# Moving one FFN multiply to GpSimd, reordering FFN pairs around the kv groups, and splitting small loads, in a fused linear-attention and SwiGLU kernel

## The chip, the cores and the metric

The kernel runs on one core of a Trainium2 chip. Its time is in device microseconds. Engines: PE is TensorE (matmuls), PEld its weight loads, DVE VectorE, ACT ScalarE, POOL GpSimd, SP SyncE. "Span" is the time from the first to the last instruction in a trace; the timed result is about 1.8 us longer. A program on one core has no second die to compare with; the runs used below are those marked "fast", and where it matters I also give the granted TensorE clock of the run, as a share of full speed.

## The reference, cut to what matters

```python
g = sigmoid((x * gate_w).sum(-1))                 # x: 2048 x 640
qkv = x @ wqkv                                    # 32 heads of 20
phi(t) = [softmax(t @ w_phi), softmax(-t @ w_phi)]
kv = phi(k)^T v ; z = sum(phi(k))                 # over all 2048 tokens
a = (phi(q) @ kv / (phi(q) @ z + 1e-6)) @ wo
b = (silu(x @ w_gate) * (x @ w_up)) @ w_down      # FFN, 1728 wide
out = g * a + (1 - g) * b
```

## The kernel before

The program has these stages. **Start:** wqkv (k part) is multiplied with a block-diagonal wbd, built from 36 small w_phi loads. **Phase 1:** for 16 token tiles, exp of both signs of the k features (`ek`), v, and the softmax normalisation of `ek`, done by POOL. **kv groups:** twelve PSUM accumulations over all 16 tiles. **Four blocks of 512 tokens:** pq chunks (q features, two exps each), zw (denominators), exp/psi items (DVE multiplies `eq` by a broadcast in PSUM, which a matmul with the weights `gtm` makes), oT chunks (attention output, evicted by ACT), then the final products with wo and wd. FFN work, in units called pairs (14 per block: gate matmuls, up matmuls, and the elementwise part), is spread between all these as filler.

A helper adds the semaphore waits from the tiles that an operation reads and writes. In the stretches shown below each engine's instructions start in the order in which the program issues them. FFN and pq outputs take turns on a ring of four PSUM banks (0 to 3); items and oT chunks alternate between banks 4 and 5.

```python
for i, (h, m1, p1, e0, e1) in enumerate(blk):                  # 36 small loads
    dma("act" if (i % 3 == 2) else "pool", dst, src)
dma("act", wvg[:, :, 0:D], ...)                                # 800 KB
...
for t in range(NT):                                            # phase 1
    ...                                                        # 20 matmuls, 2 exps, v copies
    for sg in range(2):                                        # DVE sum, reciprocal, then:
        poolop(lambda: pool.tensor_tensor(eka, eka, rb, ALU.mult), ...)
...
def ffn_pair(bt, k):             # and ffn_half(bt, k, which), the same in two halves
    mm_group(gap, [(wg[:, c, P*k:P*k+rk], xT[:, c, tsl]) for c in range(5)])
    mm_group(uap, [(wu[:, c, P*k:P*k+rk], xT[:, c, tsl]) for c in range(5)])
    actop(hap, gap, ACTF.Tanh, scale=0.5)
    dveop(... hap = (hap + 1.0) * gap ...)         # scalar_tensor_tensor, gap in PSUM
    dveop(... hap = (hap * 0.5) * uap ...)         # scalar_tensor_tensor, uap in PSUM
...
for k in range(6):
    kv_group(*kvg.pop(0))
    kv_group(*kvg.pop(0))
    ffn_pair(0, k)
...
for bt in range(NBT):
    halves = [(k, w) for k in range(6 if bt == 0 else 0, 14) for w in range(2)]
    # nh() emits the next half, if any is left
    pq_chunk 0, pq_chunk 1, nh(), pq_chunk 2, nh(), ... pq_chunk 5, nh(), nh()
    zw_groups, zw_ops, 4 x nh(), zw_transposes, 2 x nh()
    12 exp_psi_items, nh() after every second one
    6 ot_chunks, nh() after each
    while halves: nh()
    u_loop(bt, buf)              # wo and wd matmuls, combine, store
```

The softmax here doesn't subtract the row's maximum and nothing guards it: scores larger than these inputs give would overflow.

Of the kernel before, what the change touches and what calls it, by code (L numbers as in the profile page):

```python
# [6 lines left out]
P = 128  # L7
# [9 lines left out]
ACTF = mybir.ActivationFunctionType  # L17
ALU = mybir.AluOpType
AX = mybir.AxisListType
DT = mybir.dt  # L20
BF16 = DT.bfloat16
# [170 lines left out]
def _build(  # L192
# [11 lines left out]
    dbg=None,  # L204
):
    tr = _Tracker(nc)
    pe, act, dve, pool, sp = nc.tensor, nc.scalar, nc.vector, nc.gpsimd, nc.sync
# [7 lines left out]
    def sb(name, shape, dtype):  # L215
        t = nc.alloc_sbuf_tensor(name, list(shape), dtype)
        addr = nc.lookup_mloc(t).addr
        tr.reg_tensor(t, "sbuf", addr, shape_rowelems(shape), mybir.dt.size(dtype))
        return t
# [6 lines left out]
    wg = sb("wg", [P, 5, F_FFN], BF16)  # L226
    wu = sb("wu", [P, 5, F_FFN], BF16)
    hT = sb("hT", [P, 14, 512], BF16)
    gtm = [sb("gtm0", [P, 6, 120], BF16), sb("gtm1", [P, 6, 120], BF16)]
    msk = sb("msk", [P, 126], F32)  # L230
    SZW = sb("SZW", [P, 2, 6, 64], BF16)
# [2 lines left out]
    gs = sb("gs", [P, 2, NT], F32)  # L234
# [47 lines left out]
    def bank(b, c0, c1, rows=128):  # L282
        return ps[0:rows, b * 512 + c0: b * 512 + c1]
# [7 lines left out]
    def dma(engname, dst, src, transpose=False):  # L291
        eobj = tr.engobj[engname]

        def fn():
            if transpose:
                return eobj.dma_start(dst, src, transpose=True)
            return eobj.dma_start(dst, src)  # L297
        reads = [src] if src.tensor.name in tr.addr else []
        writes = [dst] if dst.tensor.name in tr.addr else []
        return run(engname, fn, reads=reads, writes=writes, semname="dma")  # L300

    def mm_group(out_ap, pairs):
        reads = [p[0] for p in pairs] + [p[1] for p in pairs]

        def fn():
            n = len(pairs)
            last = None
            for i, (l, r) in enumerate(pairs):
                last = pe.matmul(out_ap, lhsT=l, rhs=r, start=(i == 0), stop=(i == n - 1))  # L309
            return last  # L310
        return run("pe", fn, reads=reads, writes=[out_ap])
# [6 lines left out]
    def actop(out_ap, in_ap, func, scale=1.0):  # L318
        reads = [in_ap]
        if isinstance(scale, bass.AP):  # L320
            reads = reads + [scale]

        def fn():
            return act.activation(out_ap, in_ap, func, scale=scale)  # L324
        return run("act", fn, reads=reads, writes=[out_ap])

    def dveop(fn, reads, writes):
        return run("dve", fn, reads=reads, writes=writes)

    def poolop(fn, reads, writes):  # L330
        return run("pool", fn, reads=reads, writes=writes)

    def memset(t_ap, val, eng="pool"):
        eobj = pool if eng == "pool" else dve
        return run(eng, lambda: eobj.memset(t_ap, val), reads=[], writes=[t_ap])  # L335
# [18 lines left out]
    for i, (h, m1, p1, e0, e1) in enumerate(blk):  # L354
        dst = wbd[p1:p1 + (e1 - e0), m1, DH * h:DH * h + DH]
        src = wphi[h, e0:e1, :]
        dma("act" if (i % 3 == 2) else "pool", dst, src)
    dma("act", wvg[:, :, 0:D], A_wqkv[:, 2 * D:3 * D].rearrange("(c p) j -> p c j", p=P))
    gate_ap = bass.AP(gate_w.tensor, gate_w.offset, [[1, P], [P, 5], [1, 1]])
    with nc.allow_non_contiguous_dma(reason="gate_w column load (640 elems)"):  # L360
# [116 lines left out]
    def ring_next():  # L477
        i = ring_ctr[0] % 4
        ring_ctr[0] += 1
        return i  # L480

    def nrows_f(k):
        return 128 if k < 13 else 64

    def ffn_pair(bt, k):
        tsl = slice(512 * bt, 512 * bt + 512)
        rk = nrows_f(k)
        rg = ring_next()
        gap = bank(rg, 0, 512, rows=rk)
        mm_group(gap, [(wg[:, c, P * k:P * k + rk], xT[:, c, tsl]) for c in range(5)])  # L490
        ru = ring_next()
        uap = bank(ru, 0, 512, rows=rk)
        mm_group(uap, [(wu[:, c, P * k:P * k + rk], xT[:, c, tsl]) for c in range(5)])
        hap = hT[0:rk, k, :]
        actop(hap, gap, ACTF.Tanh, scale=0.5)
        dveop(lambda hap=hap, gap=gap: dve.scalar_tensor_tensor(
            out=hap, in0=hap, scalar=1.0, in1=gap, op0=ALU.add, op1=ALU.mult),
            [hap, gap], [hap])
        dveop(lambda hap=hap, uap=uap: dve.scalar_tensor_tensor(
            out=hap, in0=hap, scalar=0.5, in1=uap, op0=ALU.mult, op1=ALU.mult),  # L500
            [hap, uap], [hap])

    def kv_group(c, sg):
        nr, nk = _nr(c), _nk(c)
        ncol = 21 * nk
# [15 lines left out]
        z1 = oav[:, :, DH:DH + 1]  # L521
        dveop(lambda zdst=zdst, z0=z0, z1=z1: dve.tensor_tensor(zdst, z0, z1, ALU.mult),
              [z0, z1], [zdst])

    kvg = [(c, sg) for c in range(6) for sg in range(2)]
    for k in range(6):
        kv_group(*kvg.pop(0))
        kv_group(*kvg.pop(0))
        ffn_pair(0, k)
    assert not kvg  # L530
    if dbg is not None:
        dump_names1 = ["d_ek", "d_v1", "d_krec", "d_kvsb", "d_SZW", "d_gs"]
    else:
        dump_names1 = []

    def dump_list(names):
        if dbg is None:
            return
        dmap = {
            "d_xT": lambda: xT[:, :, :],  # L540
            "d_wqk": lambda: wqk[:, :, :, :],
            "d_wvg": lambda: wvg[:, :, :],
            "d_ek": lambda: ek[:, :, :, :],
            "d_v1": lambda: v1[:, :, :],
            "d_krec": lambda: krec[:, :, :, :],
            "d_gs": lambda: gs[:, :, :],
            "d_kvsb": lambda: kvsb[0:40, :, 0:40],
            "d_SZW": lambda: SZW[0:120, :, 0:5, :],
            "d_c36": lambda: c36[0:64, :, :],
            "d_hT": lambda: hT[0:64, :, :],  # L550
            "d_eq": lambda: eq[0:40, :, :, :, :],
            "d_oT": lambda: oT[0:40, :, :, :],
            "d_ag": lambda: ag[:, :, :],
        }
        for name in names:
            if name in dbg:
                ev = dma("sp", dbg[name], dmap[name]())
                out_evs.append(ev)
    dump_list(dump_names1)

    for bf_ in range(2):
        memset(oT[:, bf_, 5, :], 0.0)
        for sg in range(2):
            memset(eq[:, bf_, sg, 5, :], 0.0)
    memset(c36[:, :, :], 0.0)

    zwv = ps[0:P, 6 * 512:7 * 512].rearrange("p (u s c) -> p u s c", u=4, s=2)
    sub_ctr = [0]
# [73 lines left out]
    def ffn_half(bt, k, which):  # L642
        tsl = slice(512 * bt, 512 * bt + 512)
        rk = nrows_f(k)
        if which == 0:
            rg = ring_next()
            gap = bank(rg, 0, 512, rows=rk)
            mm_group(gap, [(wg[:, c, P * k:P * k + rk], xT[:, c, tsl]) for c in range(5)])
            ffn_half.gate[k] = gap
            return  # L650
        gap = ffn_half.gate[k]
        ru = ring_next()
        uap = bank(ru, 0, 512, rows=rk)
        mm_group(uap, [(wu[:, c, P * k:P * k + rk], xT[:, c, tsl]) for c in range(5)])
        hap = hT[0:rk, k, :]
        actop(hap, gap, ACTF.Tanh, scale=0.5)
        dveop(lambda hap=hap, gap=gap: dve.scalar_tensor_tensor(  # L657
            out=hap, in0=hap, scalar=1.0, in1=gap, op0=ALU.add, op1=ALU.mult),
            [hap, gap], [hap])
        dveop(lambda hap=hap, uap=uap: dve.scalar_tensor_tensor(  # L660
            out=hap, in0=hap, scalar=0.5, in1=uap, op0=ALU.mult, op1=ALU.mult),
            [hap, uap], [hap])
    ffn_half.gate = {}

    def u_loop(bt, buf):
        for u in range(4):
# [33 lines left out]
    def pq_chunk(bt, buf, m):  # L700
# [5 lines left out]
        actop(eq[0:nr, buf, 0, m, :], oap, ACTF.Exp, scale=1.0)  # L706
        actop(eq[0:nr, buf, 1, m, :], oap, ACTF.Exp, scale=-1.0)

    for bt in range(NBT):
        buf = bt % 2  # L710
        par = bt % 2
        if bt == 0:
            halves = [(k, w) for k in range(6, 14) for w in range(2)]
        else:
            halves = [(k, w) for k in range(14) for w in range(2)]

        def nh():
            if halves:
                ffn_half(bt, *halves.pop(0))

        pq_chunk(bt, buf, 0)
        pq_chunk(bt, buf, 1)
        nh()
        pq_chunk(bt, buf, 2)
        nh()
        pq_chunk(bt, buf, 3)
        nh()
        pq_chunk(bt, buf, 4)
        nh()
        pq_chunk(bt, buf, 5)  # L730
        nh(); nh()
        zw_groups(bt, buf)
        zw_ops(par)
        nh(); nh(); nh(); nh()
        zw_transposes(par)
        nh(); nh()
        items = [(sg, m) for sg in range(2) for m in range(6)]
        for it_i, it in enumerate(items):
            exp_psi_item(bt, buf, par, *it)
            if it_i % 2 == 1:  # L740
                nh()
        for m in range(6):
            ot_chunk(bt, buf, m)
            nh()
        while halves:
            nh()
        u_loop(bt, buf)
# [53 lines left out]
```

## Time and profile before

Median 386.57 us of five runs (386.07 to 388.99). The profiled execution has a span of 384.8 us.

| read from the trace of before | value |
|---|---|
| first PE matmul | 19.16 us |
| first phase-1 matmul | 27.95 us |
| PE idle before the first kv group | 3.45 us |
| exp/psi stretch of blocks 1 to 3 (first gtm to first oT matmul) | 11.47 us each |
| block 0, last oT stretch (first oT to first wo matmul) | 4.68 us |

The page of before gives busy time and share of the span by engine; in its slices each digit is the busy share in tenths of one fortieth of the span, and PEclk is the granted clock in tenths.

```profile
PE 344.2 (89%) x2165; PEld 178.8 (46%) x2201; DVE 171.9 (45%) x302; ACT 127.3 (33%) x244; POOL 72.0 (19%) x105
PE   0099999879999979999989999999999999999996
...
PEclk9999999989999999999999999999999999999999
```

PE is the busy engine, so what matters is where it waits. The waits of PE, before (total us, times, longest):

```profile
PE ps L309 <- DMA wbd<-in_A_w_phi_dram: 19.2, 1, 19.2
PE ps L309 <- DVE eq L626: 5.1, 21, 1.0
PE ps L309 <- POOL ek L468: 3.4, 1, 3.4
PE ps L309 <- DVE hT L657: 2.5, 9, 0.4
PE ps L309 <- ACT oT L324: 1.1, 3, 0.7
```

The start, the exp/psi items (DVE eq), the last normalisation of phase 1 (POOL ek), the first DVE step of the FFN, and the oT evictions. The timeline of PE around the wait for POOL (start us, duration, what, count, idle before):

```profile
74.27 1.53 PE L309 MATMUL ps<-wvg,xT 128*128 128x500 bf16 x10
79.24 2.85 PE L309 MATMUL ps<-v,ek 128*120 128x126 bf16 x32 [3.45 <-POOL ek L468]
82.31 1.91 PE L309 MATMUL ps<-xT,wg 128*128 128x512 bf16 x4 [0.22 <-issue]
84.02 1.16 PE L309 MATMUL ps<-xT,wu 128*128 128x512 bf16 x4
```

From the first gate matmul on record (one of the five is missing) to the first up matmul are four matmuls and 1.71 us, 82.31 to 84.02: 0.43 us per matmul, where the same group of five later takes 1.08 us, 0.215 each. The clock by stretch says why (the number after the POOL entry is the mean granted clock):

```profile
80.00:82.00 2.00, 1.86 (x23) 1.72 (x22) 0.35 (x2) 0.00 (x0) 0.42 (x1) 0.71 0.00 0
82.00:84.00 2.00, 1.78 (x5) 0.64 (x5) 0.35 (x2) 0.00 (x0) 0.00 (x0) 0.50 0.00 0
```

DVE in block 2's exp/psi items runs without a gap:

```profile
262.09 0.69 DVE L657 SCALAR_TENSOR_TENSOR hT<-hT,ps 128x512 bf16<-128x512 bf16 x1 [0.88 <-ACT hT L324]
262.81 0.69 DVE L660 SCALAR_TENSOR_TENSOR hT<-hT,ps 128x512 bf16<-128x512 bf16 x1
263.42 2.55 DVE L626 TENSOR_TENSOR eq<-eq,ps 120x512 bf16<-120x512 bf16 x4
265.88 0.68 DVE L657 SCALAR_TENSOR_TENSOR hT<-hT,ps 128x512 bf16<-128x512 bf16 x1
```

Two FFN steps and four items take 3.79 us (262.09 to 265.88), and so does each group of four items; PE's own work in that time is 3.0 us (four items at 0.215, two halves at 1.08).

### The profile page before, as it was taken

To read this page: it belongs to the slowest core of one execution; us is meant where nothing else is said; L and a number is where in the kernel's file an instruction comes from. 1 tells how busy PE (TensorE), PEld (TensorE's weight loads), DVE (VectorE), ACT (ScalarE), POOL (GpSimd) and SP (SyncE) were. 2 spreads that over 40 slices of the span, in tenths; PEclk is the share of its full clock that TensorE was granted. 3 is DMA by queue.
4 is the path that set the end of the run, shared out by engine and by line. 5 is a ranking of instruction groups with operands and counts; after the bars stand their busy time and mean duration, and the time that the engine had idled before them with its cause. 6 is when DMAs were issued, how large, how long until landed. Compare 5 with 4: busy or idle time off the path is not lost.

```text
span 384.8 us, 5409 instructions
## 1 busy us (share of the span) xinstructions
PE 344.2 (89%) x2165; PEld 178.8 (46%) x2201; DVE 171.9 (45%) x302; ACT 127.3 (33%) x244; POOL 72.0 (19%) x105
## 2 busy tenths in 40 slices
PE   0099999879999979999989999999999999999996
PEld 0045565456644325554434455443445554434554
DVE  0006776744516850123894411268750122894311
ACT  0136777711262241143215212522341143215210
POOL 9996888830300000000000000000000000000000
PEclk9999999989999999999999999999999999999999
DMA  4999664100000000100000010000000000000001
GB/s 98 233 184 237 213 174 122 53 0 2 2 0 2 0 2 17 36 18 0 2 0 1 2 36 34 0 2 0 2 1 19 34 17 2 0 2 0 2 34 36
DMA packets 29525, 15.53 MB, mean 40 GB/s; under 512 B 19325, under 2 KB 29501, under 8 KB 29501
## 3 DMA queue, kind: packets, MB, share of 16 engines
q1 hardware_dynamic: 27097, 14.34, 14.6%
q10 hardware_dynamic: 1636, 0.83, 0.9%
q8 instruction: 18, 0.29, 0.3%
q0 software_dynamic: 768, 0.02, 0.1%
q14 instruction: 6, 0.05, 0.0%
HBM read 8.30 MB, written 2.62 MB: 28 GB/s over the span
## 4 chain that ended last, share of the span: by engine, by line
PE 74%; DVE 13%; ACT 5%; POOL 4%; issue 2%; DMA 1%; POOLq 0%
PE ps L309 73%; DVE eq L626 7%; DVE hT L657 4%; POOL wbd L297 3%; DVE hT L660 2%; ACT eq L324 2%; ACT hT L324 2%; DMA wbd<-in_A_w_phi_dram 1%; PE pst L315 1%; POOL wbd L335 1%; ACT oT L324 1%; POOL ek L468 1%; ACT ek L324 0%; DVE ocomb L694 0%; ACT wqk L324 0%
## 5 line engine op out<-in xcount | busy, mean ns | idle before, releaser
L309 PE MATMUL ps<-xT,wg 128*128 128x512 bf16 (+1 forms) x269 | 68.2, 383 | 3.2 <-DVE hT L657 2.1
L309 PE MATMUL ps<-xT,wu 128*128 128x512 bf16 (+1 forms) x273 | 69.1, 380 | 0.4
L324 ACT ACTIVATE hT<-ps 128x512 bf16<-128x512 f32 (+1 forms) x56 | 33.4, 596 | 90.4 <-PE ps L309 90.4
L309 PE MATMUL ps<-wd,hT 128*128 128x128 bf16 (+1 forms) x440 | 62.5, 297 | 0.4
L657 DVE SCALAR_TENSOR_TENSOR hT<-hT,ps 128x512 bf16<-128x512 bf16 (+1 forms) x50 | 34.2, 684 | 62.9 <-ACT hT L324 62.9
L694 DVE SCALAR_TENSOR_TENSOR ocomb<-ps,gs,ag 128x640 bf16<-128x640 f32 x16 | 14.1, 884 | 78.8 <-PE ps L309 78.8
L309 PEld LDWEIGHTS ps<-wd,hT 128*128 128x128 bf16 x448 | 35.1, 98 | 26.5
L465 DVE TENSOR_REDUCE ksum<-ek 128x32 f32<-128x640 bf16 x32 | 25.3, 791 | 42.5 <-ACT ek L324 42.5
L309 PEld LDWEIGHTS ps<-xT,wu 128*128 128x128 bf16 (+1 forms) x280 | 27.3, 99 | 32.5 <-issue 3.0
L468 POOL TENSOR_TENSOR ek<-ek,krec 128x640 bf16<-128x640 bf16 x32 | 39.9, 1269 | 10.5 <-ACT gtan L324 10.5
L309 PEld LDWEIGHTS ps<-xT,wg 128*128 128x128 bf16 (+1 forms) x280 | 25.9, 99 | 34.0 <-PE ps L309 5.7
L324 ACT ACTIVATE eq<-ps 120x512 bf16<-120x512 f32 (+1 forms) x48 | 26.0, 593 | 29.4 <-PE ps L309 29.4
L660 DVE SCALAR_TENSOR_TENSOR hT<-hT,ps 128x512 bf16<-128x512 bf16 (+1 forms) x50 | 34.3, 686 | 1.7
L324 ACT ACTIVATE ag<-ps,gs 128x640 bf16<-128x640 f32 x16 | 12.7, 793 | 64.8 <-PE ps L309 64.8
L309 PE MATMUL ps<-wbd,wqT 128*128 128x320 bf16 (+2 forms) x65 | 13.6, 352 | 19.2 <-DMA wbd<-in_A_w_phi_dram 19.2
L626 DVE TENSOR_TENSOR eq<-eq,ps 120x512 bf16<-120x512 bf16 (+1 forms) x48 | 30.5, 680 | 0.0
L309 PE MATMUL ps<-wo,oT 120*128 120x512 bf16 (+3 forms) x188 | 28.6, 297 | 1.3 <-ACT oT L324 0.7
L309 PE MATMUL ps<-xT,wqk 128*120 128x512 bf16 (+1 forms) x120 | 29.2, 379 | 0.0
L324 ACT ACTIVATE ek<-ps 128x640 bf16<-128x640 f32 x32 | 20.8, 701 | 14.4 <-PE ps L309 14.4
L309 PE MATMUL ps<-wvg,xT 128*128 128x500 bf16 (+1 forms) x160 | 24.5, 299 | 0.0
L309 PE MATMUL ps<-wqk,xT 128*128 128x512 bf16 (+1 forms) x154 | 23.4, 296 | 1.2 <-ACT wqk L324 0.9
L324 ACT ACTIVATE oT<-ps 120x512 bf16<-120x512 f32 (+1 forms) x24 | 14.3, 596 | 23.3 <-PE ps L309 23.3
(59 smaller groups left out, 252.4 us busy)
## 6 DMA issues: line engine op xcount, KB each, us to landing
out_dram<-ocomb SPq DMA_DIRECT2D x16, 160.0 KB, 1.8
wg<-in_B_w_gate_dram SPq DMA_DIRECT2D x4, 540.0 KB, 4.3
wu<-in_B_w_up_dram SPq DMA_DIRECT2D x4, 540.0 KB, 3.8
wd<-in_B_w_down_dram SPq DMA_DIRECT2D x1, 2080.0 KB, 12.8
wvg<-in_A_wqkv_dram ACTq DMA_DIRECT2D x1, 800.0 KB, 7.2
wo<-in_A_wo_dram SPq DMA_DIRECT2D x1, 750.0 KB, 6.7
wbd<-in_A_w_phi_dram POOLq DMA_DIRECT2D x18, 0.8 KB, 4.5
wqT<-in_A_wqkv_dram SPq DMA_TRANSPOSE x10, 3.4
```

What stands on the lines that cost most here:

```text
L297: return eobj.dma_start(dst, src)
L309: last = pe.matmul(out_ap, lhsT=l, rhs=r, start=(i == 0), stop=(i == n - 1))
L315: return pe.transpose(out_ap, in_ap, ident[:, :])
L324: return act.activation(out_ap, in_ap, func, scale=scale)
L335: return run(eng, lambda: eobj.memset(t_ap, val), reads=[], writes=[t_ap])
L465: dveop(lambda eka=eka, sa=sa: dve.tensor_reduce(sa, eka, AX.X, ALU.add), [eka], [sa])
L468: poolop(lambda eka=eka, rb=rb: pool.tensor_tensor(eka, eka, rb, ALU.mult), [eka, ra], [eka])
L626: dveop(lambda ea=ea, oap=oap: dve.tensor_tensor(ea, ea, oap, ALU.mult), [ea, oap], [ea])
L657: dveop(lambda hap=hap, gap=gap: dve.scalar_tensor_tensor(out=hap, in0=hap, scalar=1.0, in1=gap, op0=ALU.add, op1=ALU.mult), [hap, gap], [ ...
L660: dveop(lambda hap=hap, uap=uap: dve.scalar_tensor_tensor(out=hap, in0=hap, scalar=0.5, in1=uap, op0=ALU.mult, op1=ALU.mult), [hap, uap], ...
L694: dveop(lambda oc=oc, b_ap=b_ap, omg=omg, aga=aga: dve.scalar_tensor_tensor(out=oc, in0=b_ap, scalar=omg, in1=aga, op0=ALU.mult, op1=ALU.add),
```

## The change

Its intent: take the second FFN step off DVE (ACT copies the up result out of PSUM, POOL multiplies in SBUF), use FFN work to cover the wait for the last normalisation, keep more FFN filler for block 0, and share the small loads evenly between two issuing engines.

```diff
+    us2 = sb("us2", [P, 2, 512], BF16)
...
-        dma("act" if (i % 3 == 2) else "pool", dst, src)
+        dma("act" if (i % 2 == 1) else "pool", dst, src)
...          # in ffn_half; ffn_pair now calls ffn_half twice
+        usa = us2[0:rk, k % 2, :]
         actop(hap, gap, ACTF.Tanh, scale=0.5)
+        actop(usa, uap, ACTF.Copy, scale=0.5)
         dveop(... hap = (hap + 1.0) * gap ...)
-        dveop(... hap = (hap * 0.5) * uap ...)
+        poolop(lambda: pool.tensor_tensor(hap, hap, usa, ALU.mult), ...)
...
-    for k in range(6):
-        kv_group(*kvg.pop(0))
-        kv_group(*kvg.pop(0))
-        ffn_pair(0, k)
+    ffn_pair(0, 0)
+    ffn_pair(0, 1)
+    for k in range(2, 8):
+        kv_group(*kvg.pop(0))
+        kv_group(*kvg.pop(0))
+        if k == 4:
+            ffn_pair(0, 2)
...
-            halves = [(k, w) for k in range(6, 14) for w in range(2)]
+            halves = [(k, w) for k in range(3, 14) for w in range(2)]
```

More of the change, by code (lines that the diff above doesn't have):

```diff
@@ L483, in nrows_f @@
         return 128 if k < 13 else 64
-    def ffn_pair(bt, k):
-        tsl = slice(512 * bt, 512 * bt + 512)
-        rk = nrows_f(k)
-        rg = ring_next()
-        gap = bank(rg, 0, 512, rows=rk)
-        mm_group(gap, [(wg[:, c, P * k:P * k + rk], xT[:, c, tsl]) for c in range(5)])
-        ru = ring_next()
-        uap = bank(ru, 0, 512, rows=rk)
-        mm_group(uap, [(wu[:, c, P * k:P * k + rk], xT[:, c, tsl]) for c in range(5)])
-        hap = hT[0:rk, k, :]
-        actop(hap, gap, ACTF.Tanh, scale=0.5)
-        dveop(lambda hap=hap, gap=gap: dve.scalar_tensor_tensor(
-            out=hap, in0=hap, scalar=1.0, in1=gap, op0=ALU.add, op1=ALU.mult),
-            [hap, gap], [hap])
-        dveop(lambda hap=hap, uap=uap: dve.scalar_tensor_tensor(
-            out=hap, in0=hap, scalar=0.5, in1=uap, op0=ALU.mult, op1=ALU.mult),
-            [hap, uap], [hap])
     def kv_group(c, sg):
@@ L523, in kv_group @@
               [z0, z1], [zdst])
-    kvg = [(c, sg) for c in range(6) for sg in range(2)]
-    for k in range(6):
-        kv_group(*kvg.pop(0))
-        kv_group(*kvg.pop(0))
-        ffn_pair(0, k)
-    assert not kvg
-    if dbg is not None:
-        dump_names1 = ["d_ek", "d_v1", "d_krec", "d_kvsb", "d_SZW", "d_gs"]
-    else:
-        dump_names1 = []
-    def dump_list(names):
-        if dbg is None:
-            return
-        dmap = {
-            "d_xT": lambda: xT[:, :, :],
-            "d_wqk": lambda: wqk[:, :, :, :],
-            "d_wvg": lambda: wvg[:, :, :],
-            "d_ek": lambda: ek[:, :, :, :],
-            "d_v1": lambda: v1[:, :, :],
-            "d_krec": lambda: krec[:, :, :, :],
-            "d_gs": lambda: gs[:, :, :],
-            "d_kvsb": lambda: kvsb[0:40, :, 0:40],
-            "d_SZW": lambda: SZW[0:120, :, 0:5, :],
-            "d_c36": lambda: c36[0:64, :, :],
-            "d_hT": lambda: hT[0:64, :, :],
-            "d_eq": lambda: eq[0:40, :, :, :, :],
-            "d_oT": lambda: oT[0:40, :, :, :],
-            "d_ag": lambda: ag[:, :, :],
-        }
-        for name in names:
-            if name in dbg:
-                ev = dma("sp", dbg[name], dmap[name]())
-                out_evs.append(ev)
-    dump_list(dump_names1)
-    for bf_ in range(2):
-        memset(oT[:, bf_, 5, :], 0.0)
-        for sg in range(2):
-            memset(eq[:, bf_, sg, 5, :], 0.0)
-    memset(c36[:, :, :], 0.0)
     zwv = ps[0:P, 6 * 512:7 * 512].rearrange("p (u s c) -> p u s c", u=4, s=2)
@@ L659, in ffn_half, with ffn_pair @@
             [hap, gap], [hap])
-        dveop(lambda hap=hap, uap=uap: dve.scalar_tensor_tensor(
-            out=hap, in0=hap, scalar=0.5, in1=uap, op0=ALU.mult, op1=ALU.mult),
-            [hap, uap], [hap])
+        poolop(lambda hap=hap, usa=usa: pool.tensor_tensor(hap, hap, usa, ALU.mult),
+               [hap, usa], [hap])
     ffn_half.gate = {}
+    def ffn_pair(bt, k):
+        ffn_half(bt, k, 0)
+        ffn_half(bt, k, 1)
     def u_loop(bt, buf):
@@ L707, in pq_chunk, with dump_list @@
         actop(eq[0:nr, buf, 1, m, :], oap, ACTF.Exp, scale=-1.0)
+    kvg = [(c, sg) for c in range(6) for sg in range(2)]
+    ffn_pair(0, 0)
[5 more added lines that the diff above has]
+            ffn_pair(0, 2)
+    assert not kvg
+    if dbg is not None:
+        dump_names1 = ["d_ek", "d_v1", "d_krec", "d_kvsb", "d_SZW", "d_gs"]
+    else:
+        dump_names1 = []
+    def dump_list(names):
+        if dbg is None:
+            return
+        dmap = {
+            "d_xT": lambda: xT[:, :, :],
+            "d_wqk": lambda: wqk[:, :, :, :],
+            "d_wvg": lambda: wvg[:, :, :],
+            "d_ek": lambda: ek[:, :, :, :],
+            "d_v1": lambda: v1[:, :, :],
+            "d_krec": lambda: krec[:, :, :, :],
+            "d_gs": lambda: gs[:, :, :],
+            "d_kvsb": lambda: kvsb[0:40, :, 0:40],
+            "d_SZW": lambda: SZW[0:120, :, 0:5, :],
+            "d_c36": lambda: c36[0:64, :, :],
+            "d_hT": lambda: hT[0:64, :, :],
+            "d_eq": lambda: eq[0:40, :, :, :, :],
+            "d_oT": lambda: oT[0:40, :, :, :],
+            "d_ag": lambda: ag[:, :, :],
+        }
+        for name in names:
+            if name in dbg:
+                ev = dma("sp", dbg[name], dmap[name]())
+                out_evs.append(ev)
+    dump_list(dump_names1)
+    for bf_ in range(2):
+        memset(oT[:, bf_, 5, :], 0.0)
+        for sg in range(2):
+            memset(eq[:, bf_, sg, 5, :], 0.0)
+    memset(c36[:, :, :], 0.0)
     for bt in range(NBT):
```

## The prediction

> **What bounds it now.** TensorE: 344 of 384.8 us busy, and it carries 74% of the chain of waits. It loses time in four places.
> (a) Start: nothing until 19.16 us, waiting for the last small wbd load (longest PE wait, 19.2 us).
> (b) Between phase 1 and the kv groups: the timeline shows PE's last phase-1 matmuls around 75.8 us and the first kv group at 79.24, the second at 80.47, each waiting for a POOL normalisation of ek. Afterwards matmuls are slow: 128x512 matmuls start 0.43 us apart at 82.3 to 84 us, against 0.215 later. This agrees with the Trainium skill, "TensorE: Matmul & The Clock Gate", Part 1 (half clock after an idle window).
> (c) The exp/psi stretch of each token block: DVE alternates hT and eq work without a gap (block 2: DVE 11.8 of 12.0 us at 262 to 274), PE waits for eq.
> (d) Block 0's six oT chunks without FFN filler: PE and ACT alternate, 139.4 to 144.1 us.
>
> **What changes.** wbd loads: POOL issues 18 instead of 24 (0.51 us each), ACT 18 instead of 12 (about 0.46). FFN: the second DVE step (0.69 us, x56) becomes an ACT copy (0.6 us) plus a POOL multiply; ek's multiply on POOL takes 1.27 us for 640 columns, so I estimate 1.05 us for 512. POOL is idle then. The skill ("GPSIMD Engine Reference", 3.1) calls two-input work there about twice as slow as on DVE; off the chain that costs little. Order: two FFN pairs before the kv groups, one amid them, eleven in block 0. PE work is unchanged.
>
> **Critical path, by place.**
> (a) POOL's issues end 3 us earlier, but the DMA engines are busy at 9 to 25 us, landing takes 4 to 7 us, and the 800 KB wvg load now starts nearer these loads. xT lands near 25 us in any case. Gain 0.8 us (0 to 2).
> (b) Two pairs (4.3 us) fill the gap from 75.8 to 80.1; their banks are free in time and POOL is then ready. PE stays at full clock. Per chunk count, block 0 should begin 4.3 us earlier than before (allowing for the three pairs moved).
> (c) DVE loses three 0.69-us steps per stretch; PE work (9 us) becomes the near-equal limit, so I take 1.65 us per block: 6.6 us over four, of which block 0's is counted with (d).
> (d) Four of six oT chunks get fillers. (c) and (d) together for block 0: 3.3 us.
> Against this: before the wd matmuls of blocks 1 and 3, the last hT row now goes copy, then POOL, ending about 0.35 us after the wo matmuls that cover it: -0.7 us. The ACT copies in the pq stretches fit into ACT's idle time: 0.
> Sum: 0.8 + 4.3 + 3.3 + 3 x 1.65 - 0.7 = 12.6 us.
>
> **Predicted 374.0 us**, 371 to 378.5. Faster by over 2% (below 378.8): 0.90; within 2%: 0.09; slower: 0.01.
>
> **What would show it.** (a) first PE matmul near 18.4. (b) no PE wait for POOL ek over 0.5 us, no 0.43-us spacing after the start. (c) the wait for DVE eq falls from 5.1 us to under 2.5; DVE total falls by about 38 us, ACT rises by about 33, POOL by about 59. (d) the wait for ACT oT falls from 1.1. New: a short PE wait for POOL hT, twice.
>
> **What would make it wrong.** POOL multiplies much longer than 1.1 us, or slowing DVE[...]; in-order ACT holding exp or oT evictions behind a copy that waits for the up matmuls; wvg landing late enough to hold up ACT's first evictions; the DVE saving hidden because PE waits for the tanh, DVE, bank-release chain instead.

## The result

The kernel after: 373.24 us median of nine runs (372.16 to 373.89), against 386.77 us (385.83 to 388.99, 15 runs) for before. The ratio is 0.9639, with a 95% interval of 0.9617 to 0.9661. Ratios here are the mean time of one kernel's fast runs over that of the other's fast runs of the same rounds, so not quite the ratio of the medians.

The page of after, same lines:

```profile
PE 340.3 (92%) x2166; PEld 177.9 (48%) x2201; DVE 134.0 (36%) x246; ACT 158.1 (43%) x300; POOL 133.2 (36%) x155
PE   0289999999999999999999999999999999999996
...
PEclk9999999999999999999999999999999999999999
```

The waits of PE, after:

```profile
PE ps L310 <- DMA wbd<-in_A_w_phi_dram: 17.1, 2, 15.6
PE ps L310 <- DVE hT L600: 2.5, 9, 0.4
PE ps L310 <- POOL hT L603: 0.9, 2, 0.5
PE ps L310 <- ACT wqk L325: 0.9, 1, 0.9
PE ps L310 <- ACT oT L325: 0.7, 1, 0.7
```

The waits for DVE eq and POOL ek are gone; a new one for POOL hT appears, twice. PE's timeline between phase 1 and the kv groups:

```profile
74.37 1.24 PE L310 MATMUL ps<-xT,wg 128*128 128x512 bf16 x5
...
77.61 1.24 PE L310 MATMUL ps<-xT,wu 128*128 128x512 bf16 x5
78.68 5.50 PE L310 MATMUL ps<-v,ek 128*120 128x126 bf16 x96
84.23 1.02 PE L310 MATMUL ps<-xT,wg 128*128 128x512 bf16 x4
```

No idle time, and no slow matmuls. DVE in block 2's items, after:

```profile
250.80 0.69 DVE L600 SCALAR_TENSOR_TENSOR hT<-hT,ps 128x512 bf16<-128x512 bf16 x1 [2.33 <-ACT hT L325]
251.46 1.29 DVE L567 TENSOR_TENSOR eq<-eq,ps 120x512 bf16<-120x512 bf16 x2
252.97 1.29 DVE L567 TENSOR_TENSOR eq<-eq,ps 120x512 bf16<-120x512 bf16 x2 [0.23 <-PE ps L310]
254.18 0.68 DVE L600 SCALAR_TENSOR_TENSOR hT<-hT,ps 128x512 bf16<-128x512 bf16 x1
```

DVE now sometimes waits for PE; a group takes 3.38 us. The start of PE shows two waits instead of one:

```profile
15.63 2.29 PE L310 MATMUL ps<-wbd,wqT 128*128 128x512 bf16 x5 [15.63 <-DMA wbd<-in_A_w_phi_dram]
19.41 0.80 PE L310 MATMUL ps<-wbd,wqT 128*128 128x128 bf16 x3 [1.49 <-DMA wbd<-in_A_w_phi_dram]
```

Marks in the two traces account for the whole difference of 13.97 us. Three pairs moved from the kv stretch into block 0 are worth 6 x 1.08 = 6.48 us of PE time, and are allowed for:

| stretch | before, us | after, us | difference, pairs allowed for |
|---|---|---|---|
| up to the first phase-1 matmul | 27.95 | 26.69 | -1.26 |
| from there to block 0's first pq matmul | 76.13 | 64.19 | -5.46 |
| to block 0's first wd matmul | 41.67 | 44.71 | -3.44 |
| to block 1's first wd matmul | 71.98 | 70.84 | -1.14 |
| to block 2's | 72.23 | 70.70 | -1.53 |
| to block 3's | 71.77 | 70.63 | -1.14 |
| to the end | 23.11 | 23.11 | 0.00 |

### The profile page after: what moved, and what is told of

The parts are those of the page before. It is cut to its first block, busy times and chain, and to the rows that moved or that the text cites. A ratio compares the mean times of both kernels' runs of the same rounds, so it can differ in the third digit from the quotient of the medians.

```text
span 370.9 us, 5518 instructions
## 1 busy us (share of the span) xinstructions
PE 340.3 (92%) x2166; PEld 177.9 (48%) x2201; DVE 134.0 (36%) x246; ACT 158.1 (43%) x300; POOL 133.2 (36%) x155
## 4 chain that ended last, share of the span: by engine, by line
PE 85%; ACT 4%; POOL 3%; issue 2%; DVE 2%; DMA 2%; POOLq 0%
PE ps L310 84%; POOL wbd L298 2%; ACT eq L325 2%; DMA wbd<-in_A_w_phi_dram 2%; DVE hT L600 2%; ACT hT L325 1%; PE pst L316 1%; POOL wbd L336 1%; ACT us L325 0%; POOLq L761 0%; POOL hT L603 0%; ACT oT L325 0%; DVE ocomb L640 0%; ACT wqk L325 0%; POOLq L123 0%
## 5 line engine op out<-in xcount | busy, mean ns | idle before, releaser
L603 POOL TENSOR_TENSOR hT<-hT,us 128x512 bf16<-128x512 bf16 (+1 forms) x56 | 64.2, 1151 | 198.2 <-DVE hT L600 142.6
L600 DVE SCALAR_TENSOR_TENSOR hT<-hT,ps 128x512 bf16<-128x512 bf16 (+1 forms) x56 | 37.8, 683 | 92.6 <-ACT hT L325 92.6
L310 PE MATMUL ps<-xT,wg 128*128 128x512 bf16 (+1 forms) x268 | 67.1, 379 | 3.2 <-DVE hT L600 2.1
L325 ACT ACTIVATE us<-ps 128x512 bf16<-128x512 f32 (+1 forms) x56 | 33.6, 601 | 25.3 <-PE ps L310 24.8
L310 PE MATMUL ps<-wbd,wqT 128*128 128x320 bf16 (+2 forms) x65 | 14.4, 363 | 17.1 <-DMA wbd<-in_A_w_phi_dram 17.1
L310 PE MATMUL ps<-wvg,xT 128*128 128x500 bf16 (+1 forms) x160 | 24.5, 299 | 0.0
```

The costliest lines, as they stand in the source:

```text
L310: last = pe.matmul(out_ap, lhsT=l, rhs=r, start=(i == 0), stop=(i == n - 1))
L325: return act.activation(out_ap, in_ap, func, scale=scale)
L600: dveop(lambda hap=hap, gap=gap: dve.scalar_tensor_tensor(out=hap, in0=hap, scalar=1.0, in1=gap, op0=ALU.add, op1=ALU.mult), [hap, gap], [ ...
L603: poolop(lambda hap=hap, usa=usa: pool.tensor_tensor(hap, hap, usa, ALU.mult), [hap, usa], [hap])
```

## The experiments

My theory was that the three edits act in separate stages and add up: the loads at the start, the order before and in block 0, the split of the FFN step in the exp/psi items of all blocks. The main rivals: that one edit needs the other; that the order pays through fillers, not through the filled gap; that the split pays because the copy frees a PSUM bank earlier, not because DVE has less to do. All kernels below gave correct results. By the 2% rule of the record e1, e3, e4, e5b and e6b count as the same as before and e2 as unclear; their intervals all end below 1, and what each edit is worth is read from the stages. One call of four kernels came back without being run, and they went again unchanged under the labels with a "b".

### One part of the change alone: e1, e2, e3

**e1_loads_only**, before with

```diff
-        dma("act" if (i % 3 == 2) else "pool", dst, src)
+        dma("act" if (i % 2 == 1) else "pool", dst, src)
```

> Only the wbd loads are split evenly between POOL and ACT; all else is the kernel before. Theory (the four parts of the change act in separate stages and add up): first phase-1 matmul at about 26.7 us instead of 27.95, everything later shifted by that, span 1.3 us shorter, ratio 0.9967. As in the kernel after, I expect the first matmul near 15.6 us and then a second wait of about 1.5 us for a late wbd load. Rival (the start is set by when xT has landed, near 25 us, or the even split only helped because of something else in the change): span within 0.3 us of before.

Ratio 0.996 (0.9926 to 0.9994), as expected, but by itself it settles little: the spans of its five normal runs, 381.8 to 385.1 us, overlap those of before. Runs of the same granted clock say more: at 0.991 its spans are 383.2 to 385.1 us, those of before in the same call 385.8 to 386.7 (means 1.7 us apart); at 0.995 or 0.996 they are 381.8 and 384.7 against 384.2 to 384.7 (means 1.2 us apart). Its sixth run, which was the profiled one, took 1938 us (see the last section), so no stage can be read from it. The first matmul of that trace did come at 15.71 us. The worth of the loads is taken up again in e12b.

**e2_order_only**: the kernel after with the loads and the two DVE steps of before.

```diff
-        dma("act" if (i % 2 == 1) else "pool", dst, src)
+        dma("act" if (i % 3 == 2) else "pool", dst, src)
-        actop(usa, uap, ACTF.Copy, scale=0.5)
-        poolop(... hap = hap * usa ...)
+        dveop(... hap = (hap * 0.5) * uap ...)
```

> Only the order of the FFN pairs and kv groups is that of the kernel after; loads and the two DVE steps are those of before. Theory: from the end of phase 1 to block 0's first pq matmul 5.5 us are gained (gap filled and clock kept), block 0's oT stretch gains about 1.9 us from its fillers, blocks 1 to 3 keep their length. Span about 377.4 us, ratio 0.981. Rival (the early pairs need the split FFN, because two DVE steps per pair delay the release of the banks): PE waits in the kv stretch and less than 4 us are gained in all.

Ratio 0.9814 (0.9787 to 0.9841), span 378.4 us. Up to block 0 it gained 4.85 us (64.80 us for the stretch of 76.13, pairs allowed for), in block 0 1.91 us, in blocks 1 and 2 0.21 and 0, in block 3 0.01 (the 0.21 is a missing record in the trace of before, see e7b). So the order works without the split, but 0.6 us less well than in the kernel after: in the kv groups PE waited once, 0.5 us, for DVE, which still had two steps per early pair before the kv evictions. To that extent the rival is right.

**e3_split_only**: before with the copy and the POOL multiply in place of the second DVE step.

```diff
+        actop(usa, uap, ACTF.Copy, scale=0.5)
-        dveop(... hap = (hap * 0.5) * uap ...)
+        poolop(... hap = hap * usa ...)
```

> Only the second FFN step is moved from DVE to an ACT copy and a POOL multiply; loads and order are those of before. Theory: blocks 1, 2, 3 get shorter by 1.1, 1.5, 1.1 us as in the kernel after, block 0 by about 1.5, nothing before block 0. Span about 379.6 us, ratio 0.986. Rival (the split only pays once the order is changed, or the whole gain is the order): less than 2 us gained.

Ratio 0.985 (0.9818 to 0.9883), span 378.3 us. Block 0 gained 1.51 us, blocks 1 to 3 gained 1.38 (1.17 without the missing record of before), 1.54 and 1.16: as expected. But the stretch before block 0 also became 1.66 us shorter, which I had put at nothing, with the same 3.45 us of PE waiting. The clock by stretch of this trace:

```profile
80.00:82.00 2.00, 1.85 (x32) 1.70 (x31) 0.35 (x2) 0.00 (x0) 0.90 (x1) 1.00 0.00 0
82.00:84.00 2.00, 2.00 (x11) 0.92 (x9) 0.56 (x3) 0.60 (x1) 0.00 (x0) 1.00 0.00 0
```

The same wait, and the clock stayed at 1.00. In the trace of before it was 0.71, 0.50 and then 0.93 from 80 to 86 us, which loses 2 x (0.29 + 0.50 + 0.07) = 1.72 us. So the slow matmuls after the gap come in some executions and not in others. The spans of e3's four runs fit that: 378.3 at a mean clock of 1.000, 379.7 twice at 0.996, 381.0 at 0.991. Of 22 runs of before, ten had 0.995 or 0.996 (383.7 to 384.7 us) and twelve 0.991 (385.5 to 387.4 us); none had 1.000. The nine runs of the kernel after all had 0.999 or 1.000.

The traces show more of these spells. In the two in which the clock fell before the last few microseconds, it stayed at half for 3.41 us, and it fell a whole number of such steps after its first rise at the start (where the matmul spacing goes from 0.43 to 0.216 us): 17 steps after 22.83 us in before, 33 steps after 24.30 us in e5b below. The step before the fall and the spell in before:

```profile
77.44:80.86 3.42, 1.48 (x23) 1.34 (x24) 2.17 (x7) 0.41 (x3) 2.75 (x3) 1.00 0.00 0
80.86:84.27 3.41, 3.19 (x18) 1.94 (x18) 0.35 (x2) 0.01 (x1) 0.00 (x0) 0.50 0.00 0
```

So the clock fell 1.6 us after the wait had ended, at the end of a step, and the same wait can lie differently across the steps when the start shifts. That this decides whether the clock falls is not shown, and PE's busy time in the step does not decide it alone: 1.48 us before the fall in before, 2.00 in e5b, but 1.49 and 1.74 in the two steps around e3's wait, which kept the clock. A spell costs half of its 3.41 us, 1.7 us; over a span of 385 us, one gives a mean clock of 0.996 and two give 0.991, the classes seen above.

The three ratios multiply to 0.996 x 0.9814 x 0.985 = 0.963; the whole change measured 0.964. The parts add up within their intervals (about 0.003 either way for each).

### What the filled gap is worth: e4, e5b

**e4_two_ahead** fills the gap but leaves block 0 as it was.

```diff
+    ffn_pair(0, 0)
+    ffn_pair(0, 1)
     for k in range(6):
         kv_group(*kvg.pop(0))
         kv_group(*kvg.pop(0))
-        ffn_pair(0, k)
+        if k < 4:
+            ffn_pair(0, k + 2)
```

> The kernel before with two FFN pairs moved ahead of the kv groups, the other four left between the kv groups, block 0 unchanged (pairs 6 to 13). It takes the filled gap alone, without the fillers for the oT chunks. Theory: 5.5 us gained between the end of phase 1 and block 0, nothing after it: span about 379.3 us, ratio 0.986, no matmul spacing of 0.43 us after 30 us. Rival (the gain of the order comes mainly from leaving eleven pairs to block 0, i.e. from fillers): under 3 us gained.

Ratio 0.9852 (0.9819 to 0.9885), granted clock 0.999 or 1.000 in all four runs. The stretch before block 0 fell from 76.13 to 70.62 us, 5.51 us less; block 0 kept its length (41.70). So the gap is worth 5.5 us against an execution with the slow clock, of which about 1.7 us is the clock, and the 1.9 us in block 0 of e2 come from the fillers.

**e5b_one_ahead**: one pair ahead, `ffn_pair(0, 0)` before the loop and `if k < 5: ffn_pair(0, k + 1)` in it.

> The kernel before with one FFN pair ahead of the kv groups (five between them). The pair takes 2.15 us, so about 1.3 us of waiting for the first ek multiply and 0.3 for the second remain. Theory (what costs most there is the wait itself, and the half clock follows only a wait as long as the 3.4 us of before): no slow matmuls, granted clock 0.999 or 1.0 in every run, span about 1.6 us longer than with two pairs ahead, near 381.8 us. Rival (any wait of this size lets the clock drop): granted clock of 0.991 to 0.996 in most runs, as in before, and span 383 us or more.

PE waited 1.3 us, as expected, and there was no slow matmul after it. Three of the four runs had a clock of 1.000 and spans of 381.0 to 381.8 us. The profiled run had 0.995 and 382.9 us, and its slow spell was elsewhere, in block 0's oT stretch, where no FFN filler was left. The step before it is the end of the exp/psi stretch, where PE waited 1.0 us and twice 0.2 us for DVE eq:

```profile
133.53:136.94 3.41, 2.00 (x8) 0.59 (x6) 3.38 (x6) 0.00 (x0) 0.00 (x0) 1.00 0.00 0
136.94:140.35 3.41, 3.41 (x9) 1.10 (x8) 0.17 (x1) 1.97 (x4) 0.00 (x0) 0.50 0.00 0
```

The oT stretch took 5.60 us there, 0.92 more than before's 4.68, and block 0 as a whole was 0.95 us longer than before's. The theory held for this wait. Its forecast of a full clock in every run failed, and so did the rival's of a low clock in most runs: stretches without one long wait can lose the clock too. Runs of before at 0.991 have lost the time of two spells; that these are the one of before and the one of e5b is a guess, since no run of before at 0.991 was profiled.

### DVE, POOL and the banks: e6b, e7b

**e6b_dve_second**: the kernel after, the second multiply on DVE, from the copy in SBUF. The bank is released by the copy as in the kernel after.

```diff
-        poolop(lambda: pool.tensor_tensor(hap, hap, usa, ALU.mult), ...)
+        dveop(lambda: dve.tensor_tensor(hap, hap, usa, ALU.mult), ...)
```

> The kernel after, but the second multiply is done by DVE from the copy in SBUF instead of by POOL. Banks are released as early as in the kernel after; only the DVE work comes back, in part. The Trainium skill (VectorE: DVE Perf Modes, Rules for kernel authors) gives a 16-bit two-input op in SBUF twice the rate, so I estimate 0.35 us per step instead of 0.69. Theory (the stretch of exp/psi items is set by DVE's sum): the stretch from the first gtm matmul to the first oT matmul grows from 9.9 to about 10.5 us per block, the two POOL waits of 0.45 us vanish, span about 372 us. With a step of 0.6 us it would be 375. Rival (the gain came from the early release of the banks by the ACT copy): the stretch stays at 9.9 us and the span falls to 370.

This was far off: span 379.9 us, ratio to before 0.9856 (0.9821 to 0.9892). The step was short, 0.43 us, yet the exp/psi stretch took 12.0 us per block, longer than before's 11.47. The twofold rate that the Trainium skill ("VectorE: DVE Perf Modes", Rules for kernel authors) gives for a 16-bit two-input op in SBUF agrees in direction: 0.43 us against 0.68 for the step from PSUM that was replaced, 1.6 times, though the two are not the same operation. DVE in block 2 of e6b:

```profile
256.07 0.69 DVE L600 SCALAR_TENSOR_TENSOR hT<-hT,ps 128x512 bf16<-128x512 bf16 x1 [1.40 <-ACT hT L325]
257.22 0.42 DVE L603 TENSOR_TENSOR hT<-hT,us 128x512 bf16<-128x512 bf16 x1 [0.46 <-ACT us L325]
257.56 2.55 DVE L567 TENSOR_TENSOR eq<-eq,ps 120x512 bf16<-120x512 bf16 x4
260.02 0.68 DVE L600 SCALAR_TENSOR_TENSOR hT<-hT,ps 128x512 bf16<-128x512 bf16 x1
```

DVE stands still for 0.46 us until ACT's copy is there, and the eq multiplies that PE needs are behind it in program order. A group of four items takes 3.95 us. I had added up DVE's work and left out that it would wait, in order, for a result two engines away. The experiment refutes the rival (early bank release with DVE still in the loop gains nothing in this stretch) and sharpens the theory: the gain is that DVE neither does the step nor waits for its input. The wait before the wd matmuls did vanish, as expected.

**e7b_pool_twice**: the kernel after with an idle POOL multiply, us2 by itself into a scratch tile, before each real one.

> The kernel after with a second, useless POOL multiply of the same size before each real one (POOL work for the FFN doubles, about 64 us more). Theory (POOL is off the chain except for the last row of hT before the wd matmuls): 1.15 us more in blocks 1 and 3 each and about 0.4 in block 2, span near 373.6 us, ratio to the kernel after about 1.007. Rival (POOL already sets the pace somewhere): more than 5 us longer.

Spans 372.6 to 375.2 us, ratio to before 0.9698. With 56 more POOL multiplies of 1.03 us, the exp/psi stretch is the same 9.93 us. The distances from the first wo to the first wd matmul in blocks 1 to 3 were 2.97, 2.50 and 2.97 us. In the kernel after they are 2.0, 1.6 and 2.0 (read in e12b, which shares this part: 2.03, 1.63, 2.04; in the traces of before and after the record of the first wd matmul is missing in these blocks, which makes those marks 0.2 us late in both). So each grew by about 0.9 us. PE's waits for POOL:

```profile
PE ps L311 <- POOL hT L607: 3.0, 3, 1.2
```

That is the place where the theory put POOL on the chain, but not the only one. The stretch from the first pq to the first gtm matmul also grew, from 24.70 to 24.89 us in blocks 1 to 3, because POOL held up DVE in the zw part, which ends with two DVE steps that make `ctok`:

```profile
176.88 1.04 POOL L605 TENSOR_TENSOR scr<-us 128x512 bf16<-128x512 bf16 x1 [3.14 <-ACT us L326]
177.12 0.95 DVE L552 TENSOR_TENSOR ctok<-zsb,zwt 128x128 bf16<-128x128 f32 x1
178.10 0.29 DVE L553 TENSOR_TENSOR ctok<-zsb,zwt 128x128 bf16<-128x128 f32 x1
```

In all four blocks the ctok step that ran beside a POOL multiply took 0.94 or 0.95 us, the other 0.29; PE's transposes of `ctok` then start about 0.2 us later. Both inputs of that step are in SBUF. In e6b, too, the one DVE multiply of hT by us2 that ran beside a POOL multiply took 0.79 us instead of 0.43. DVE steps with one input in PSUM are not longer beside POOL: the eq multiplies of after take 0.68 us, the 28 beside a POOL multiply and the 12 others.

### The start: e12b, e8

**e12b_old_loads**: the kernel after with `i % 3 == 2` again.

> The kernel after with the wbd loads split as before (every third to ACT). This asks for the worth of the loads where the clock stays full all along. Theory (additive parts): first phase-1 matmul at about 28 us instead of 26.7, span about 1.3 us longer than the kernel after, near 372.2 us. Rival (the start varies from run to run by as much as the loads are worth): spans overlap those of the kernel after, 370.4 to 372.1 us.

Six runs, all at 0.999 or 1.000: spans 371.9 to 373.0 us, against 370.4 to 372.1 for the nine runs of the kernel after, which ran on another occasion. The medians, 372.8 and 371.5, are 1.3 us apart, and the ranges just overlap. In the traces that keep after's loads and leave wvg where it was, the first phase-1 matmul came at 26.69, 27.76, 27.59, 26.99 and 25.62 us (after, e6b, e7b, e9, e10), mean 26.9; with the old loads at 27.95, 28.28, 28.43, 28.82, 28.91 and 28.59 (before, e2, e3, e4, e5b, e12b), mean 28.5. The even split is worth about 1.5 us, and the start varies by 1 to 2 us by itself.

**e8_wvg_first**: the kernel after with the 800 KB wvg load first on ACT's queue, before all others.

> The kernel after with the 800 KB wvg load issued first of all on ACT's queue (about 0.8 us) instead of behind ACT's wbd loads (11.8 us). In the kernel after, the last wbd load lands at 19.2 us, 6.5 us after its issue, while wvg is moving; PE starts at 15.6 and then waits a second time. Theory (that second wait comes from the wvg transfer competing with the last wbd loads): with wvg out of the way the second wait disappears or shrinks under 0.5 us, the first phase-1 matmul comes near 24.5 us instead of 26.7 to 27.8, span about 369 us. Rival (POOL's issue queue or the transposes set it): the second wait stays over 1 us and the span within 0.7 us of the kernel after.

PE started at 16.47 us, and the second wait was gone. Phase 1 began at 25.98 us, not at 24.5, because the first matmuls now ran at half clock in the chain; in the kernel after some of them ran during the wait. The last small load was issued by POOL at 12.62 us in e8 and at 12.63 in after, and landed at 17.10 instead of 19.17, so POOL's issue queue is not the cause. Spans 368.6 to 370.1 us, median 369.3 against 371.5 for the kernel after on another occasion; the two profiled starts are only 0.7 us apart (25.98 and 26.69), the later stretches equal. So the late second wait of the kernel after does come from the wvg transfer beside the last small loads.

### What still holds PE: e9, e10, and all together in e11

**e9_last_row_dve**: in blocks 1 to 3, row k = 13 keeps the old DVE step from PSUM.

```diff
+        if k == 13 and bt > 0:       # no copy for this row either
+            dveop(... hap = (hap * 0.5) * uap ...)
+            return
```

> The kernel after, but in blocks 1 to 3 the last hT row (k = 13) takes the old second DVE step from PSUM, without copy and POOL. Theory (the new wait before the wd matmuls is that row's copy and POOL multiply): the distance from the first wo to the first wd matmul in blocks 1 and 3 falls from 2.0 to 2.3 us to about 1.8, no PE wait for POOL hT remains, span 0.4 to 0.9 us shorter, near 370.6. Rival (something else holds the wd matmuls): the distance stays.

The distance from the first wo to the first wd matmul in blocks 1 and 3 fell from 2.0 to 1.65 us, and no wait for POOL hT is left. Spans 368.6 to 370.8 us, median 370.45. The gain of 0.4 us twice is read from the stages; the whole time alone would not show it.

**e10_gate_early**: for the pairs among the pq chunks, tanh and the first DVE step are emitted right after the gate matmuls.

```diff
     if which == 0:
         mm_group(gap, ...)
+        if early:
+            actop(hap, gap, ACTF.Tanh, scale=0.5)
+            dveop(... hap = (hap + 1.0) * gap ...)
         return
```

> The kernel after, but for the FFN pairs among the pq chunks the tanh and the first DVE step are issued right behind the gate matmuls instead of behind the up matmuls. It tests what still holds PE in that stretch (2.5 us of waits for DVE hT in the trace of after, plus the idle weight loads there). Theory (in-order ACT runs the exps of a later chunk before the tanh, so the gate bank is released late): the stretch from the first pq to the first gtm matmul falls from 24.7 to about 23.4 us per block, span about 5 us shorter, near 366 us. Rival (these waits are hidden behind other limits of the stretch, such as ACT's total): less than 2 us gained.

The wait for DVE hT fell from 2.5 us to 0.4:

```profile
PE ps L310 <- DVE hT L609: 0.4, 1, 0.4
```

The stretch from the first pq to the first gtm matmul fell from 24.7 to 23.95 us in blocks 1 to 3, 0.75 us each where I expected 1.3. In the trace of after, two gate groups of such a stretch start 0.48 and 0.28 us late (1.56 us after the preceding group instead of 1.08, and 1.47 instead of e10's 1.19); I had read the idle time of the weight loads (0.75 and 0.67 us) as if it were PE's. Spans 366.8 to 369.0 us.

**e11_all**: e8, e9 and e10 together.

> The kernel after with all three: wvg first, last row on DVE, gate early. If they add up: about 363 us, ratio to the kernel after about 0.977.

Six runs, 367.64 us median, ratio to before 0.9491 (0.946 to 0.9522). Over the kernel after that is 0.9491 / 0.9639 = 0.985, from runs of different occasions, and a smaller gain than the 0.977 I expected. The measured parts add up: 2.2 us (e8) + 4 x 0.75 (e10) + 0.8 (e9) from 371.5 us gives 365.5, and the median span is 365.8. That fit is partly luck, since the 2.2 us of e8 is a difference between occasions and its stages show 0.7. By stages, the traces of after and e11 are 4.98 us apart: 1.1 at the start, 3.0 in the pq stretches, 0.8 before the wd matmuls. What failed was the estimate of e10. This version beats both kernels.

## Why the prediction was right

The time, 373.24 us against 374.0 predicted, is within the range, and the reasons hold in the main. Point by point:

- **(a) start, predicted gain 0.8 us, first PE matmul near 18.4.** The gain was 1.26 us in the two traces and about 1.5 us in the means over all traces. The picture was wrong, and the near size was luck: the first group needs only the earlier loads and started at 15.63, and PE then waited a second time, until 19.41, for a load that landed at 19.17 (in before PE's only wait ended with a landing at 18.92). The gain is that five half-clock matmuls ran before that. e8 shows that the second wait is owed to the wvg transfer.
- **(b) gap, predicted 4.3 us, measured 5.46.** The mechanism is right (e4). In the trace of before the wait of 3.45 us, another 0.30 before the second kv group and 1.71 of lost clock make up the 5.46. The prediction took the 4.3 us of the two pairs for the whole: more than the waits (3.75), and no term for the clock. It also left out that the lost clock is not there in every execution (e3).
- **(c) exp/psi stretch, predicted 1.65 us per block, measured 11.47 - 9.93 = 1.54.** Right, and e6b shows more than the prediction knew: DVE's place in the chain counts as well as its busy time.
- **(d) with block 0's share of (c), predicted 3.3 us, measured 3.44.** Right; e2 and e3 divide it into 1.9 (fillers) and 1.5 (split).
- **The new wait, predicted 0.35 us in blocks 1 and 3.** The distances from wo to wd rose by 0.40 us in both and by nothing in block 2 (marks of before and after: 1.86 to 2.26, 1.85 to 1.86, 1.86 to 2.26). e9 removes it and e7b lengthens it.
- **Busy totals.** DVE fell by 37.9 us (predicted 38), ACT rose by 30.8 (33), POOL by 61.2 (59). The POOL multiply took 1.15 us, estimated 1.05:

```profile
L603 POOL TENSOR_TENSOR hT<-hT,us 128x512 bf16<-128x512 bf16 (+1 forms) x56 | 64.2, 1151 | 198.2 <-DVE hT L600 142.6
L600 DVE SCALAR_TENSOR_TENSOR hT<-hT,ps 128x512 bf16<-128x512 bf16 (+1 forms) x56 | 37.8, 683 | 92.6 <-ACT hT L325 92.6
```

DVE's step is as long as before (0.684 us), so POOL beside it did not slow this step, which has one input in PSUM. The prediction's risk that POOL slows DVE is real for steps with both inputs in SBUF (e7b), but in the kernel after none of the zw steps ran beside a POOL multiply. The longer POOL step costs only in the two waits above.

## What to carry to other kernels

Read an engine's place in the chain, not its share of busy time: POOL's slow multiply (1.15 us) beat DVE's fast one (0.43 us), because the fast one made an in-order DVE wait for a copy, with urgent work queued behind it. Put independent matmuls into a wait of PE: the wait goes, and so does the half clock that sometimes follows it. Look too at what runs beside the engine that takes over the work: a DVE step with both inputs in SBUF took 0.95 us instead of 0.29 beside POOL. When a kernel's times fall into classes, look at the granted clock of each run before explaining them.

## What the Trainium skill lacked or had wrong

- "TensorE: Matmul & The Clock Gate", Part 1, lets the clock fall after an idle window of about 3.4 us and calls the window free-running. The traces agree on the window: the spells last 3.41 us and lie whole steps from the first rise, and 3.45 us of waiting gave half clock in one trace and none in another. They differ on idle: neither fall followed a window without work, for PE was busy 1.48 us of it in before and 2.00 in e5b, where its longest wait was 1.0 us. A later passage of that part does name frequent short idles between groups of matmuls, but not how much of them is enough; the runs do not settle that either.
- The same part puts the ramp at the start under 1% of a typical kernel. The traces agree: in before it lost about 1.8 us of 385 (half of 19.16 to 22.83 us). The spells in mid-kernel stay under that as well: mean clocks of 0.996 and 0.991 went with spans 1.4 and 2.7 us over the one at 1.000 (e3: 379.7 and 381.0 against 378.3), up to 0.7%: small, but as large as several of the effects studied.
- "GPSIMD Engine Reference", 4.1, gives GpSimd as about twice as slow for two-input elementwise work. Here POOL took 1.15 us, DVE 0.43 us for the same 16-bit multiply in SBUF (2.7 times), and DVE 0.68 us for the step from PSUM that it replaced (1.7 times).
- No page that I read has a whole execution like this: one of e1 took 1938 us, with 128x512 matmuls starting 1.28 us apart instead of 0.216 (5.9 times), correct results, and ACT and DVE at their usual durations (an exp of ek still 1.30 us for two). The nearest is a remark in the Part 1 named above, of a clock gate stuck at a quarter. The trace holds no clock event, where each of the other 13 holds at least two, so the 1.00 listed as its granted clock is no measurement, and whether PE's clock was the cause stays open. The other five runs of that kernel were normal. The line of PE's groups in that trace (busy, mean ns):

```profile
L309 PE MATMUL ps<-xT,wu 128*128 128x512 bf16 x260 | 359.2, 1688 | 0.0
```
